# Keeping the exchange buffers of one more batch on chip in a fused Fourier-mixing and mixture-of-experts kernel

## The chip, the cores and the metric

The kernel runs on one core of a Trainium2 chip. The metric is the device time of one execution in microseconds (us); lower is better. The kernel before takes 1597.15 us, the median of three runs (1596.53 to 1599.73). Its trace comes from a further execution under the profiler, which took longer: 1614.27 us, of which 1612.5 us lie between the first and the last instruction. All times below that carry a position ("at 131.87") are positions in that trace.

## The reference

Two layers in a row, all in float32. The first multiplies each batch (2496 tokens of 256 numbers, 8 batches) by a filter in the frequency domain. The second sends each of the 19968 tokens to the one of 8 experts with the largest gate logit.

```python
# x: (8, 2496, 256), filt: (1249, 256), w_gate: (256, 8), w1: (8, 256, 1024), w2: (8, 1024, 256)
X = np.fft.rfft(x, axis=1)
y = np.fft.irfft(X * (filt_r + 1j * filt_i)[None], n=2496, axis=1)
t = y.reshape(19968, 256)
logits = t @ w_gate
e = argmax(logits, axis=1)                 # one expert for each token
gate = softmax(logits)[e]
out = gate * (relu(t @ w1[e]) @ w2[e])
```

## The kernel before

A batch's Fourier transform of length 2496 = 39 x 64 is done as four sets of small matrix products, which the kernel calls stages. Stage A transforms along 39 (tokens on the partitions), stage B along 64 and then multiplies by the filter, stage C transforms back along 64, stage D back along 39. Between A and B, and between C and D, the data change their layout. For batches 1 to 7 this is done by way of DRAM: the result of A is stored to `zd` and loaded again in another order, the result of C likewise through `ud`.

```python
def load_z(b, c):                          # DRAM -> SBUF, ahead of stage B
    f0, n = FH[c]
    zi = fin(("z", b, c))
    nc.sync.dma_start(out=zi[:HP, :n], in_=zd[b][:, f0:f0 + n, :])
    nc.sync.dma_start(out=zi[HP:, :n], in_=zd[b][:, NF + f0:NF + f0 + n, :])

def stage_a(b, c):                         # two groups of tokens per product
    ...
    for j in range(0, n, 2):
        p = bank()
        mm(p[:TK, :], lhsT=tas, rhs=xt[:TP, j:j + 2, :], start=True, stop=True)
        evac(zo[:, j:j + 2, :], ...)       # PSUM -> SBUF, on VectorE or ScalarE
    for r, m, v in columns(zd[b], i0, n):
        move(v, zo[:r, m])                 # SBUF -> DRAM

def stage_b(b, f):
    c, j = divmod(f, 4)
    if b == 0:
        zi, j = outs.pop(("zi", f)), 0
    else:
        zi = ins["z", b, c] if j == 0 else ins.pop(("z", b, c))
    p = bank()
    mm(p, lhsT=tbs, rhs=zi[:, j:j + 2, :], start=True, stop=True)
    ...
    nc.vector.tensor_mul(ys, z2, ht[:, f:f + 2, :])
    nc.vector.scalar_tensor_tensor(out=yw[:HP], in0=z2[HP:], scalar=-1.0, in1=fi, ...)
    nc.vector.tensor_mul(yw[HP:], z2[:HP], fi)
    (nc.gpsimd if b == 0 else nc.vector).tensor_tensor(ys, ys, yw, op=ALU.add)
```

Stage C is one product of 512 columns per step and ends in `move` to `ud`; stage D reads `ud` back through `load_u`.

Batch 0 is treated differently: its data stay in SBUF, in two buffers `zt` and `ut`, and the layout is changed by TensorE transposes against the identity.

```python
def first_a(c):                            # stage A of batch 0
    ...
    for j in range(0, n, 2):
        p = bank()[:, :4 * TK]
        for h in range(DH):
            for i in range(2):
                mm(p[...], lhsT=xt[:TP, j + i, h * P:(h + 1) * P], rhs=tas, start=True, stop=True)
        for h in range(DH):
            evac(zv[:, h], pv[:, h], 2 * TK)             # into zt

def turn_z(f):                             # between A and B of batch 0
    ...
    for i in range(2):
        for h in range(DH):
            nc.tensor.transpose(p[:, i, h, :], zu["z"][:, h, f + i]..., ident)
    evac(zi, p..., 2 * D)

def first_c(f):                            # stage C of batch 0: four products of 128 columns
    ...
    for h in range(DH):
        evac(zu["u"][:, h, :, :, f:f + 2], ..., D)       # into ut

def turn_u(c):                             # between C and D of batch 0: four transposes, one evac
    ...
```

After stage D of a batch, its logits are taken (`turn_y`, `logits`, `turn_logits`), its tokens are routed on VectorE (`route`) and scattered by GpSimd to a DRAM list sorted by expert (`rows`). The experts read 256 or 512 rows of that list at a time (`turn_x`, `hidden` or `hidden_by_quarters`, `result`), with the weights of that expert loaded for each such tile. For tiles of 512 rows GpSimd adds blocks of the rows (`sums`) and of the weights (`wsum`) first.

The program is built by a list of steps. Slot k holds stages B and C of batch k, stage A of batch k + 1 and stage D of batch k - 1. Steps of the experts are put between those of the slots by an estimate of time that the builder keeps. The order on each engine is then fixed. The experts' SBUF pool takes the place of batch 0's pool `pro`, so it opens when batch 0 has done with it, in slot 1:

```python
def experts_pool():
    first.close()
    pools["moe"] = ctx.enter_context(tc.tile_pool(name="moe", bufs=2, side="right", reuse_waits="tile"))

# in slot(k), for k > 0
    for c in range(nch + 3):
        at = 0.45 * c / (nch + 3) - 0.1 if k == 1 else 0.2 + 0.8 * c / (nch + 3)
        if c < nch and k == 1:
            steps.append((at - 0.05, lambda c=c: turn_u(c), None, 0.22 * CH[c][1]))
        ...
        if k == 1 and c == nch:
            steps.append((at, experts_pool, None, 0.0))
    steps.append((0.38 if k == 1 else 2.0, lambda: begin_route(k - 1), None, 0.0))
```

Lines of the kernel that the profile names: L413 `first_a`, L430 `turn_z`, L438 `first_c`, L453 `turn_u`, L337 `stage_a`, L351 the product of `stage_b` and L358 to L362 its filter, L372 `stage_c`, L391 and L395 `stage_d`, L466 `turn_y`, L480 `logits`, L491 `turn_logits`, L537 and L538 products of `route`, L596 the scatter to `rows`, L727 `turn_x`, L743 to L746 `wsum`, L765 `hidden_by_quarters`, L806 `hidden`, L821 `result`, L227 every `evac`.

Of the kernel before, what the change touches and what calls it, by code (L numbers as in the profile page):

```python
# [10 lines left out]
F32 = mybir.dt.float32  # L11
# [8 lines left out]
P = 128  # L20
S = 2496
D = 256
# [5 lines left out]
N2 = 64  # L28
# [90 lines left out]
def kernel(  # L119
# [174 lines left out]
    ins, outs, lgs, yts = {}, {}, {}, {}  # L294
    NIN, YB = 7, 6

    moves, stored = [[], []], set()

    def move(o, i):
# [43 lines left out]

    def stage_b(b, f):
        c, j = divmod(f, 4)
        if b == 0:
            zi, j = outs.pop(("zi", f)), 0
        else:
            zi = ins["z", b, c] if j == 0 else ins.pop(("z", b, c))
        p = bank()  # L350
        mm(p, lhsT=tbs, rhs=zi[:, j:j + 2, :], start=True, stop=True)  # L351

        z2 = p.rearrange("p (i d) -> p i d", i=2)
        ys = outs["y", b, f] = sb.tile([P, 2, D], F32, tag="ys", name="ys", bufs=3)
        yw = (pro if b == 0 else sb).tile([P, 2, D], F32, tag="yw", name="yw", bufs=2 if b == 0 else 1)
        half, f1 = divmod(f, NF // 2)
        fi = ht[half * HP:(half + 1) * HP, NF + f1:NF + f1 + 2, :]
        nc.vector.tensor_mul(ys, z2, ht[:, f:f + 2, :])  # L358
        nc.vector.scalar_tensor_tensor(out=yw[:HP], in0=z2[HP:], scalar=-1.0, in1=fi, op0=ALU.mult, op1=ALU.mult)
        nc.vector.tensor_mul(yw[HP:], z2[:HP], fi)  # L360

        (nc.gpsimd if b == 0 else nc.vector).tensor_tensor(ys, ys, yw, op=ALU.add)  # L362
        free["v"] = max(free["v"], now[0]) + (2.1 if b == 0 else 2.8)
# [17 lines left out]
    def stage_d(b, c):  # L381
        if c == 0:
            lgs[b] = sb.tile([TP, NG, E], F32, tag="lg", name="lg")
        i0, n = CH[c]
        held_y[0] += 1
        ui = outs.pop(("ui", c)) if b == 0 else ins.pop(("u", b, c))
        yo = outs["o", b, c] = sb.tile([P, 4, DR], F32, tag="y", name="yo", bufs=YB)[:TP]
        for j in range(0, n, 2):
            p = bank()
            if i0 + j + 2 < NG:  # L390
                mm(p[:TP, :], lhsT=tds, rhs=ui[:TK, j:j + 2, :], start=True, stop=True)  # L391
            else:

                for i, k in enumerate((TK, NS)):
                    mm(p[:TP, i * D:(i + 1) * D], lhsT=tds[:k, :], rhs=ui[:k, j + i, :], start=True, stop=True)  # L395
            evac(yo[:, j:j + 2, :D], p[:TP, :].rearrange("p (i d) -> p i d", i=2), 512)
# [2 lines left out]

    zu = {}  # L400

    def first_a(c):
        i0, n = CH[c]
        xt = ins.pop(("x", 0, c))
        if c == 0:

            zu["z"] = pro.tile([P, DH, NF, 2, N2], F32, name="zt", bufs=1)
            zu["u"] = pro.tile([P, DH, N2, 2, NF], F32, name="ut", bufs=1)
        for j in range(0, n, 2):
            p = bank()[:, :4 * TK]  # L410
            for h in range(DH):
                for i in range(2):
                    mm(p[:, (2 * h + i) * TK:(2 * h + i + 1) * TK], lhsT=xt[:TP, j + i, h * P:(h + 1) * P], rhs=tas,  # L413
                       start=True, stop=True)
            t0 = NB * (i0 + j)
            m = min(2 * NB, N2 - t0)
            pv = p.rearrange("p (h t c f) -> p h c f t", h=DH, c=2, f=NF)[:, :, :, :, :m]
            zv = zu["z"].rearrange("p h f c t -> p h c f t")[:, :, :, :, t0:t0 + m]
            for h in range(DH):
                evac(zv[:, h], pv[:, h], 2 * TK)  # L420

    def turn_z(f):
        if f % 4 == 0:
            nc.scalar.copy(out=ht[HP:, f:f + 4], in_=ht[:HP, f:f + 4])
            free["s"] = max(free["s"], now[0]) + 1.1
        zi = outs["zi", f] = pro.tile([P, 2, D], F32, tag="zi", name="zi")
        p = bank().rearrange("p (i h d) -> p i h d", i=2, h=DH)
        for i in range(2):
            for h in range(DH):
                nc.tensor.transpose(p[:, i, h, :], zu["z"][:, h, f + i].rearrange("p c t -> p (c t)"), ident)  # L430
        evac(zi, p.rearrange("p i h d -> p i (h d)"), 2 * D)

    def first_c(f):
        ys = outs.pop(("y", 0, f))
        p = bank().rearrange("p (h i c t) -> p h i c t", h=DH, c=2, i=2)
        for i in range(2):
            for h in range(DH):
                mm(p[:, h, i].rearrange("p c t -> p (c t)"), lhsT=ys[:, i, h * P:(h + 1) * P],  # L438
                   rhs=tcs, start=True, stop=True)
        for h in range(DH):  # L440
            evac(zu["u"][:, h, :, :, f:f + 2], p[:, h].rearrange("p i c t -> p t c i"), D)

    def turn_u(c):
        i0, n = CH[c]
        ui = outs["ui", c] = pro.tile([P, 4, D], F32, tag="ui", name="ui")
        for j in range(0, n, 2):
            p = bank().rearrange("p (i h d) -> p i h d", i=2, h=DH)
            whole = i0 + j + 2 < NG
            for i in range(2):
                t0 = NB * (i0 + j + i)  # L450
                m = min(NB, N2 - t0)
                for h in range(DH):
                    nc.tensor.transpose(  # L453
                        p[:m * NS, i, h, :], zu["u"][:, h, t0:t0 + m].rearrange("p t c f -> p (t c f)"), ident)
                if not whole:
                    evac(ui[:m * NS, j + i, :], p[:m * NS, i].rearrange("p h d -> p (h d)"), D)
            if whole:
                evac(ui[:TK, j:j + 2], p[:TK].rearrange("p i h d -> p i (h d)"), 2 * D)
# [380 lines left out]
    def slot(k):  # L839

        steps, nch = [], len(CH)
        if k == 0:
            steps.append((0.4, load_rest, None, 0.0))
            for f in range(-2, NF + 2, 2):
                at = (f + 2) / (NF + 4)
                if 0 <= f < NF:
                    steps.append((at, lambda f=f: stage_b(k, f), None, 0.85))
                if f + 2 < NF:
                    steps.append((at + 0.01, lambda f=f: turn_z(f + 2), None, 0.44))
                if f >= 2:  # L850
                    steps.append((at + 0.02, lambda f=f: first_c(f - 2), None, 0.85))
        elif k < B:
            for f in range(0, NF + 2, 2):
                at = f / (NF + 2)
                if f < NF:
                    steps.append((at, lambda f=f: stage_b(k, f), ("z", k, f // 4) if f % 4 == 0 else None, 0.85))
                if f >= 2:
                    steps.append((at + 0.01, lambda f=f: stage_c(k, f - 2), None, 0.85))
        if k + 1 < B:
            for c in range(nch):  # L860
                steps.append(((0.25 if k == 0 else 0.0) + 0.7 * c / nch, lambda c=c: stage_a(k + 1, c), ("x", k + 1, c), 0.43 * CH[c][1]))
        if k > 0:
            for c in range(nch + 3):
                at = 0.45 * c / (nch + 3) - 0.1 if k == 1 else 0.2 + 0.8 * c / (nch + 3)
                if c < nch and k == 1:
                    steps.append((at - 0.05, lambda c=c: turn_u(c), None, 0.22 * CH[c][1]))
                if c < nch:
                    steps.append((at, lambda c=c: stage_d(k - 1, c), ("u", k - 1, c) if k > 1 else "y", 0.43 * CH[c][1]))
                if c >= 3 and c % 2:
                    steps.append((at + 0.01, lambda c=c: logits(k - 1, (c - 3) // 2), None, 0.9))  # L870
                if 1 <= c <= nch:
                    steps.append((at + 0.03, lambda c=c: turn_y(k - 1, c - 1), None, 0.22 * CH[c - 1][1]))
                if c >= 3 and c % 2:
                    later = at + (0.07 if k == 1 else 0.11)
                    steps.append((later, lambda c=c: turn_logits(k - 1), None, 0.25))
                    steps.append((later + 0.001, lambda c=c: sides.append(route(k - 1, (c - 3) // 2)), None, 0.0))
                if k == 1 and c == nch:
                    steps.append((at, experts_pool, None, 0.0))
            steps.append((0.38 if k == 1 else 2.0, lambda: begin_route(k - 1), None, 0.0))
        return sorted(steps, key=lambda step: step[0])  # L880

    STEPS = [(0.0, lambda: load_filters(0), None, 0.0)]
    for c in range(len(CH)):
        STEPS.append((0.0, lambda c=c: first_a(c), ("x", 0, c), 0.43 * CH[c][1]))
        if c + 1 < len(FH):
            STEPS.append((0.0, lambda c=c: load_filters(c + 1), None, 0.0))
    SLOT = []
# [182 lines left out]
```

## Time and profile before

| what | value |
|---|---|
| time, median of 3 | 1597.15 us |
| span of the profiled execution | 1612.5 us |
| TensorE, matmul records | 1536.1 us, 95%, 7432 records |
| VectorE / ScalarE / GpSimd busy | 43% / 33% / 38% |
| moved by DMA | 287.50 MB, 178 GB/s over the span |
| `fin<-zd`, `zd<-zo`, `ud<-uo`, `fin<-ud` | loads and stores of the exchange, 7 batches |

A float32 product appears as two matmul records, a transpose as one. The records of one engine can overlap, since a product starts before the last one has drained; a record's duration is therefore longer than the time by which it moves the next one back. "Waited for" names what released an engine after it stood idle. PE is TensorE, PEld its weight loads, DVE VectorE, ACT ScalarE, POOL GpSimd, SP the queue from which the DMAs are issued.

### The profile page before, as it was taken

How to read it: one execution, taken by the hardware profiler on the slowest of the kernel's cores; microseconds unless marked ns; L12 is line 12 of the kernel's file. 1: busy time of each engine (PE TensorE's matmuls, PEld its weight loads, DVE VectorE, ACT ScalarE, POOL GpSimd, SP SyncE). 2: the span in 40 equal slices, each digit the busy share in tenths (PEclk: the TensorE clock that was granted, in tenths of full speed). 3: DMA queues.
4: the chain of work that ended last, by engine and by line, in shares of the span. 5: the costliest groups of instructions: out<-in, count | busy, mean ns of one | idle time of the engine just before them, and what ended most of it. 6: DMA issues, size and time to landing. Idle time of an engine off the chain costs nothing. (4 is left out here: it accounts for less than half of the span.)

```text
span 1612.5 us, 23212 instructions
## 1 busy us (share of the span) xinstructions
PE 1536.1 (95%) x7432; PEld 1211.1 (75%) x7432; DVE 694.7 (43%) x1797; ACT 533.5 (33%) x1106; POOL 608.5 (38%) x715
## 2 busy tenths in 40 slices
PE   7988898999999999999999899988999999999998
PEld 5533556667678767887688687877888888899997
DVE  4676562443756565357646354336343420000000
ACT  4434342343332333333333332222322223333433
POOL 4132324213634553455435555564444411111111
PEclk9999898999999999999999999999999999999999
DMA  8669695596784485446634633343344447665561
GB/s 245 166 193 300 217 328 164 180 314 217 206 264 142 153 270 156 121 139 163 195 116 141 165 127 115 116 160 102 99 165 139 164 144 249 194 230 179 171 190 34
DMA packets 119276, 287.50 MB, mean 178 GB/s; under 512 B 17587, under 2 KB 58812, under 8 KB 119157
## 3 DMA queue, kind: packets, MB, share of 16 engines
q1 hardware_dynamic: 99941, 242.69, 49.7%
q0 software_dynamic: 19216, 43.33, 7.9%
q8 instruction: 61, 1.00, 0.3%
q14 instruction: 58, 0.48, 0.1%
HBM read 205.95 MB, written 80.90 MB: 178 GB/s over the span
## 5 line engine op out<-in xcount | busy, mean ns | idle before, releaser
L821 PE MATMUL bank<-w2t,hT 128*128 128x256 f32 x2240 | 500.3, 380 | 0.2 <-ACT part L778 0.2
L821 PEld LDWEIGHTS bank<-w2t,hT 128*128 128x128 f32 x2240 | 424.8, 190 | 75.9 <-issue 17.2
L827 POOL DMA_INDIRECT out_dram<-ys,idt x163 | 160.8, 986 | 610.8 <-ACT ys L826 326.4
L596 POOL DMA_INDIRECT rows<-yo,row x176 | 175.0, 994 | 223.1 <-issue 54.5
L826 ACT ACTIVATE ys<-bank,gts 128x256 f32<-128x256 f32 x161 | 76.2, 474 | 425.9 <-PE bank L821 348.1
L773 ACT ACTIVATE hT<-hT 128x1024 f32<-128x1024 f32 x112 | 113.7, 1052 | 292.9 <-DVE hT L769 253.2
L806 PE MATMUL bank<-xT,w1t 128*128 128x128 f32 (+1 forms) x1184 | 191.9, 317 | 0.3 <-issue 0.3
L765 PE MATMUL bank<-sums,wsum 128*128 128x256 f32 x672 | 165.9, 393 | 19.4 <-POOL wsum L744 7.7
L806 PEld LDWEIGHTS bank<-xT,w1t 128*128 128x128 f32 x1184 | 169.3, 193 | 20.0 <-issue 9.3
L765 PEld LDWEIGHTS bank<-sums,wsum 128*128 128x128 f32 x672 | 129.7, 197 | 50.4 <-issue 10.5
L769 DVE TENSOR_TENSOR hT<-bank,part 128x512 f32<-128x512 f32 x168 | 115.6, 688 | 117.5 <-ACT part L778 63.0
L227 DVE COPY xT<-bank 128x128 f32<-128x128 f32 (+2 forms) x46 | 20.2, 439 | 286.1 <-PE bank L727 264.0
L812 ACT ACTIVATE hT<-bank 128x128 f32<-128x128 f32 (+1 forms) x295 | 93.4, 318 | 81.7 <-PE bank L806 68.2
L765 PE MATMUL bank<-xT,w1t 128*128 128x256 f32 x448 | 108.5, 386 | 0.4 <-ACT yo L227 0.4
L358 DVE TENSOR_TENSOR ys<-bank,ht 128x512 f32<-128x512 f32 x80 | 55.0, 688 | 100.4 <-PE bank L351 68.6
L765 PEld LDWEIGHTS bank<-xT,w1t 128*128 128x128 f32 x448 | 83.7, 193 | 15.3 <-issue 3.3
L372 PE MATMUL bank<-ys,tcs 128*128 128x512 f32 x140 | 75.3, 620 | 12.5 <-DVE ys L362 8.5
L769 DVE TENSOR_TENSOR part<-bank,part 128x512 f32<-128x512 f32 x112 | 76.7, 685 | 18.0 <-PE bank L765 14.5
L821 PE MATMUL bank<-w2s,hT 128*128 x368 | 83.2, 379 | 0.0
L743 POOL TENSOR_TENSOR wsum<-w1t 128x256 f32<-128x256 f32 x56 | 41.8, 747 | 106.4 <-PE bank L765 99.2
L769 DVE TENSOR_TENSOR hT<-bank,hT 128x512 f32<-128x512 f32 x112 | 76.8, 685 | 8.9 <-PE bank L765 4.2
L391 PE MATMUL bank<-fin,tds 120*117 120x512 f32 x140 | 69.6, 620 | 7.4 <-DMA fin<-ud 7.4
(152 smaller groups left out, 1813.2 us busy)
## 6 DMA issues: line engine op xcount, KB each, us to landing
w1t<-in_moe_w_dram SPq DMA_DIRECT2D x130, 512.0 KB
w2t<-in_moe_w_dram SPq DMA_DIRECT2D x84, 512.0 KB
fin<-in_x_dram SPq DMA_DIRECT2D x40, 512.0 KB
fin<-zd SPq DMA_DIRECT2D x70, 256.0 KB
ud<-uo SPq DMA_DIRECT2D x70, 256.0 KB
zd<-zo SPq DMA_DIRECT2D x35, 480.0 KB
fin<-ud SPq DMA_DIRECT2D x35, 480.0 KB
xg<-rows SPq DMA_DIRECT2D x28, 544.0 KB
```

The costliest lines, as they stand in the source:

```text
L358: nc.vector.tensor_mul(ys, z2, ht[:, f:f + 2, :])
L372: mm(p, lhsT=tcs, rhs=ys, start=True, stop=True)
L391: mm(p[:TP, :], lhsT=tds, rhs=ui[:TK, j:j + 2, :], start=True, stop=True)
L596: sc = nc.gpsimd.indirect_dma_start(out=rowsd, out_offset=bass.IndirectOffsetOnAxis(ap=at, axis=0), in_=what, in_offset=None,)
L765: mm(q[:, v], lhsT=left[:, v * P:(v + 1) * P], rhs=right, start=True, stop=True)
L769: nc.vector.tensor_tensor(o, q, a, op=ALU.add)
L773: nc.scalar.activation(o, q, AF.Relu)
L806: mm(p[:, :m], lhsT=w1t[2 * i + g][:, dh, fh, v * P:(v + 1) * P], rhs=xts[i][:, dh, :m], start=(dh == 0), stop=(dh == DH - 1))
L812: lambda: nc.scalar.activation(hT, p[:, :m], AF.Relu))
L821: mm(p[:, :D], lhsT=hs[i][k % 4 // 2][:, k // 4, k % 2, j // 2, j % 2 * P:(j % 2 + 1) * P], rhs=w2, start=(k == 0), stop=(k == FT - 1))
L826: lambda: nc.scalar.activation(ys, p[:, :D], AF.Copy, scale=gate))
L827: nc.gpsimd.indirect_dma_start(out=out, out_offset=bass.IndirectOffsetOnAxis(ap=idt[i].bitcast(U32)[:, j, :], axis=0), in_=ys, in_offset=None,
```

## The change

Batch 1 is treated as batch 0 was: its data stay in SBUF between the stages, and no longer pass through `zd` and `ud`. The two buffers `zt` and `ut` become three of the same size that are taken by turns: z of batch 0, u of batch 0, z of batch 1, and u of batch 1 in the place of z of batch 0. Since the pool `pro` is needed one batch longer, the experts' pool opens in slot 2 instead of slot 1, and the tile list of batch 0 is made then too. The purpose is to spare the early part of the kernel four passes of a batch through DRAM. The sum in the filter step stays on VectorE for batch 1.

```diff
+    CHIP = 2
 def stage_b(b, f):
-        if b == 0:
-            zi, j = outs.pop(("zi", f)), 0
+        if b < CHIP:
+            zi, j = outs.pop(("zi", b, f)), 0
...
-        yw = (pro if b == 0 else sb).tile([P, 2, D], F32, tag="yw", name="yw", bufs=2 if b == 0 else 1)
+        yw = (pro if b < CHIP else sb).tile([P, 2, D], F32, tag="yw", name="yw", bufs=2 if b < CHIP else 1)
...
+    def exchange(name, b):
+        zu[name, b] = pro.tile([P, DH * N2 * NS], F32, tag="zu", name=name, bufs=3)
...
-            zu["z"] = pro.tile([P, DH, NF, 2, N2], F32, name="zt", bufs=1)
-            zu["u"] = pro.tile([P, DH, N2, 2, NF], F32, name="ut", bufs=1)
+            exchange("z", b)
...
 (first_a, turn_z, first_c and turn_u take the batch as an argument; first_c opens u at f == 0)
...
 def slot(k):
         if k == 0:
             steps.append((0.4, load_rest, None, 0.0))
+        if k < CHIP:
             for f in range(-2, NF + 2, 2):
...
-                steps.append((..., lambda c=c: stage_a(k + 1, c), ("x", k + 1, c), 0.43 * CH[c][1]))
+                steps.append((..., lambda c=c: (first_a if k + 1 < CHIP else stage_a)(k + 1, c), ("x", k + 1, c), ...))
         if k > 0:
+            soon = k <= CHIP
             for c in range(nch + 3):
-                at = 0.45 * c / (nch + 3) - 0.1 if k == 1 else 0.2 + 0.8 * c / (nch + 3)
-                if c < nch and k == 1:
+                at = 0.45 * c / (nch + 3) - 0.1 if soon else 0.2 + 0.8 * c / (nch + 3)
+                if c < nch and soon:
...
-                if k == 1 and c == nch:
+                if k == CHIP and c == nch:
                     steps.append((at, experts_pool, None, 0.0))
+                    for b in range(CHIP - 1):
+                        steps.append((at + 0.001, lambda b=b: begin_route(b), None, 0.0))
-            steps.append((0.38 if k == 1 else 2.0, lambda: begin_route(k - 1), None, 0.0))
+            if k >= CHIP:
+                steps.append((0.45 if k == CHIP else 2.0, lambda: begin_route(k - 1), None, 0.0))
```

## The prediction

> **What bounds the kernel now.** I read the page first. Its first line says that TensorE is the engine that counts:
>
> ```profile
> PE 1536.1 (95%) x7432; PEld 1211.1 (75%) x7432; DVE 694.7 (43%) x1797; ACT 533.5 (33%) x1106; POOL 608.5 (38%) x715
> ```
>
> But 95% is a share of records that overlap. The timeline of TensorE gives what a step really takes from it: the distance from one start to the next where nothing waits.
>
> ```profile
> 33.48 1.02 PE L351 MATMUL bank<-zi,tbs 128*128 128x512 f32 x2
> 34.35 0.60 PE L430 MATMUL bank<-ident,zt 128*128 128x128 f32 x4
> 34.78 1.06 PE L438 MATMUL bank<-tcs,ys 128*128 128x128 f32 x8
> 35.67 1.88 PE L337 MATMUL bank<-fin,tas 117*120 117x512 f32 x4
> 37.39 1.02 PE L351 MATMUL bank<-zi,tbs 128*128 128x512 f32 x2
> ```
>
> A product of 512 columns (2 records) costs 34.35 - 33.48 = 0.87 us, four transposes 0.43, four products of 128 columns (8 records) 0.89, two products of stage A 1.72. Likewise the timeline gives 0.216 us for each record of 256 columns, 0.112 for one of 128 or 120, 0.100 for a transpose of 117 columns, 0.87 for the eight transposes of L453, and 0.059 for a record of L480. I multiply these by the instruction lists of the program, in their order, and cut at the last stage C product of each batch. All products together need 1486 us; the span is 1612.5. About 126 us are waits, a slow clock after them, and the two ends, and only those can be won. The view by windows, cut at the same places (columns: length, busy PE, PEld, DVE, ACT, POOL, granted clock, DMA share, GB/s), shows where they lie:
>
> ```profile
> 0.00:55.30 55.30, 45.24 (x249) 32.71 (x250) 30.32 (x56) 25.19 (x47) 23.96 (x32) 1.00 0.74 205
> 55.30:119.60 64.30, 54.93 (x234) 28.01 (x234) 44.27 (x104) 25.11 (x50) 13.03 (x13) 0.96 0.72 194
> 119.60:189.10 69.50, 59.46 (x216) 30.81 (x214) 39.53 (x121) 27.86 (x58) 17.00 (x18) 0.89 0.88 279
> 189.10:309.50 120.40, 108.78 (x453) 75.51 (x452) 58.51 (x199) 41.37 (x87) 41.20 (x45) 0.93 0.68 211
> 309.50:418.50 109.00, 105.03 (x465) 73.40 (x464) 54.62 (x161) 40.04 (x89) 37.70 (x41) 0.98 0.80 247
> 418.50:892.30 473.80, 467.61 (x2160) 359.57 (x2159) 271.75 (x637) 154.86 (x271) 224.28 (x268) 1.00 0.58 173
> 892.30:1105.00 212.70, 193.72 (x922) 160.44 (x921) 90.37 (x240) 58.35 (x100) 118.71 (x143) 0.96 0.42 131
> 1105.00:1612.50 507.50, 501.35 (x2744) 450.64 (x2742) 105.36 (x281) 160.72 (x409) 132.60 (x159) 1.00 0.50 162
> ```
>
> Window lengths less the work in them: slot 0 55.3 - 41.2 = 14.1 (5.3 of it before the first product), slot 1 64.3 - 49.3 = 15.0, slot 2 69.5 - 49.9 = 19.6, slot 3 120.4 - 99.0 = 21.4, slot 4 109.0 - 101.5 = 7.5. Slots 5 to 7 lose 13, the rest 36. The change can reach the first five: 78 us. What ends the waits there (waits of PE, first 400 us):
>
> ```profile
> PE bank L372 <- DVE ys L362: 7.8, 6, 2.7
> PE bank L765 <- POOL wsum L744: 7.7, 2, 4.7
> PE rk L537 <- DVE oe L526: 6.7, 2, 3.4
> PE bank L413 <- DMA fin<-in_x_dram: 5.3, 1, 5.3
> PE bank L727 <- DMA xg<-rows: 4.0, 1, 4.0
> PE bank L391 <- DMA fin<-ud: 2.2, 1, 2.2
> ```
>
> The reader is to see that DRAM exchange itself ends one wait of 2.2 us. More is lost to VectorE's filter and to the first expert tiles. Each wait is followed by slow products:
>
> ```profile
> 131.87 3.61 PE L391 MATMUL bank<-fin,tds 120*117 120x512 f32 x4 [2.20 <-DMA fin<-ud]
> 249.55 5.48 PE L765 MATMUL bank<-sums,wsum 128*128 128x256 f32 x12 [4.66 <-POOL wsum L744]
> ```
>
> Four records of 512 columns take 1.88 us elsewhere (L337 above), here 3.61.
>
> **What the Trainium skill says.** Perfetto Trace Analysis, section Identifying the Most-Contended Engine: busy time of matmuls is no measure of how near TensorE is to its limit, since pipelined instructions overlap. The trace agrees (1536 us busy, some 1486 of work), which is why I use start-to-start times. TensorE: Matmul & The Clock Gate, section What's actually happening: after an idle window of about 3.4 us the clock falls to half, and comes back after about as long of work. The trace agrees in kind (3.61 against 1.88 us above), though there the wait just before was only 2.20 us. The same page, section Part 4: PE-mode transpose: the result goes to PSUM and has to be copied out, and a transpose of 128x128 took about 275 ns; here the record of L430 lasts 274 ns, but the next one starts 109 ns later.
>
> **The change part by part.** *TensorE, added.* `turn_z`: 40 transposes at 0.109 = 4.4 us. `turn_u`: 44 at 0.109 = 4.8. `first_a`: 88 records at 0.112 = 9.9, in place of 22 at 0.429 = 9.4: +0.5. `first_c`: 80 at 0.112 = 9.0 in place of 20 at 0.429 = 8.6: +0.4. Stages B and D cost the same. Sum: 10.1 us and 210 more records. It is work on the engine that bounds.
>
> *DMA, removed.* z and u of one batch, 64 x 40 x 256 x 4 bytes each, stored and loaded: 4 x 2.62 = 10.5 MB. In the first 189 us the windows move 11.3 + 12.5 + 19.4 = 43 MB, so a quarter goes, and most of the direct wait of L391 (2.2 us plus 1.7 of slow clock).
>
> *ScalarE and VectorE.* 10 more evictions for `zi` at 0.587 us, 12 for `ui`, 20 of 256 elements at 0.425 instead of 10 of 0.585, 22 of 240 instead of 11 of 512. By the instruction lists VectorE gets 5 more and ScalarE 38 more: about 16 us on ScalarE, which is busy 25 of 64 us in slot 1. Beside other work.
>
> *What moves.* In the new order the first expert products come near the end of slot 2 (3.0 us of them before the last stage C of batch 2, against 5.6 before), after batch 1's scatter. The first tile of 512 rows comes with stages of batches 2 and 3 between its products, and on GpSimd its `sums` and `wsum` stand together, where before eight scatters of about 1.3 us each stood among them. The expert work by the end of slot 4 is the same in both, 115.8 us.
>
> *Slot by slot.* I take the length of a stretch from its like in the trace before. Slot 0: work 41.6, 55.5 us. Slot 1: work 54.0. Its second half is paced by VectorE: four filter operations of 0.69 to 0.72, 2.8 us per step, and the same number as before; the seven steps from 92.9 to 119.6 took 26.7 us with 18 of TensorE work in them, so the 3 us of new transposes there are free, and those in the first half are not: 66.5 us. Slot 2: work 52.7, like slot 1 before (49.3 in 64.3), with the 3 us of experts in VectorE's shadow: 64 us. It ends at 186 instead of 189.1. Slot 3: work 104.4. Of the loss of 21.4 I drop the two `wsum` waits in part (7.7 to 3), half of the slow clock after them (2 to 3), and the part due to late loads: 13 stays, 117.5 us. Slot 4: work 98.1 + 5 = 103. Sum: 406.5 against 418.5 with equal expert work done. That is 12 us; after it nothing differs by design. I take off 3 for ScalarE (second rival). 1597.15 - 9 = 1588.
>
> **Rivals.** *First, VectorE and routing keep the pace, and the added work is paid in full.* For it: `ys` L362 leads the waits, DMA ends only a small part of them, and the experts, which fill holes, come later. Then slots 1 and 2 last some 70 us each and 10 us are given away: 1603 to 1607. Against it: TensorE has 15 to 20 us of slack in each of the slots 1 to 3. *Second, ScalarE becomes the limit at the start of slot 2.* In the new order nearly all evictions of `ui`, `yo`, `yt` and `zo` there go to ScalarE, in pairs on one engine, some 25 us of them against 32 of TensorE work, in a chain of transposes, eviction, product, eviction. It would cost 3 to 8 us: 1591 to 1597. *Third, everything early is relieved.* DMA is busy 88% in slot 2 and clock is at 0.89; if the loss of slots 1 to 4 (63 us) fell to 25, the gain would be 38 - 10 = 28: 1569. Against it: the filter's waits and those of routing (`oe` L526, 6.7) stay by the lists. *Fourth, the last third shifts.* From 892 to 1105 waits cost some 25 us, two of 5.8 and 4.7 us before L765. The new order shifts them by a few us either way, with no rule that I can read.
>
> **Range and chances.** The first rival and the third are 1605 and 1569; the fourth adds 6 either way. 8 in 10: 1573 to 1603. Faster by over 2% needs less than 1565, past the third rival: 0.04. Slower by over 2% needs more than 1629, 24 us beyond the first: 0.01. Within 2%: 0.95.
>
> **What would show it.** Right: 277 MB moved and 7642 records; no `fin<-ud` wait at the first L391; last stage C of batch 2 near 186 and of batch 4 near 406; wait for `wsum` about 3 us; the stretch after the last stage C of batch 7, which was 720 us and gets 3.5 us more of expert work, within 8 us of 724. The step on slots 1 and 2 is wrong if these two together last over 138 us or under 125; that on slot 3 if its loss is still 20. The whole is wrong if the loss saved early comes back after slot 4, or if ScalarE ends more than 6 us of TensorE's waits in slot 2.

## The result and the profile after

The changed kernel takes 1623.29 us (median of 4; 1622.63 to 1624.43) where the kernel before takes 1597.16 us beside it: ratio 1.0161, 95% interval 1.0144 to 1.0179. It is 26 us slower; 1588 with a range of 1573 to 1603 had been predicted. The same program takes from 1597 to 1615 us from one chip and occasion to the next, so every ratio below is to the kernel before on the same chip in the same set of runs.

In the new kernel most lines stand 13 further down: L339 `stage_a`, L353 product of `stage_b`, L360 to L364 its filter, L374 `stage_c`, L393 `stage_d`, L424 `first_a`, L441 `turn_z`, L451 `first_c`, L466 `turn_u`, L527 to L551 `route`, L609 the scatter, L701 the load of `xg`, L740 `turn_x`, L746 to L749 `sums`, L756 to L759 `wsum`, L778 `hidden_by_quarters`, L834 `result`, L839 and L840 its eviction and the store of output rows.

The page of the changed kernel, totals and DMA:

```profile
PE 1541.9 (95%) x7642; PEld 1230.9 (76%) x7642; DVE 704.1 (43%) x1802; ACT 547.4 (34%) x1144; POOL 608.3 (37%) x715
DMA packets 112358, 277.03 MB, mean 171 GB/s; under 512 B 17067, under 2 KB 53172, under 8 KB 112237
```

Exactly 7642 records and 277 MB: what is added and removed was counted rightly. The view by windows, cut at the last stage C product of batches 0 to 4 and 7 (the sixth window is slots 5 to 7), with the columns of the prediction:

```profile
0.00:56.80 56.80, 46.85 (x316) 39.66 (x316) 31.08 (x60) 25.29 (x54) 23.93 (x32) 1.00 0.69 204
56.80:121.80 65.00, 58.77 (x333) 37.47 (x332) 46.21 (x112) 31.20 (x68) 16.73 (x16) 0.99 0.35 100
121.80:188.60 66.80, 59.45 (x254) 32.42 (x254) 41.11 (x132) 33.34 (x70) 16.85 (x17) 0.94 0.61 184
188.60:312.40 123.80, 111.36 (x475) 77.02 (x475) 55.55 (x168) 42.61 (x88) 33.48 (x39) 0.94 0.74 227
312.40:421.20 108.80, 101.84 (x449) 71.03 (x449) 59.19 (x172) 41.73 (x90) 45.03 (x49) 0.97 0.77 248
421.20:888.90 467.70, 462.80 (x2144) 356.95 (x2143) 271.08 (x638) 154.13 (x268) 222.32 (x266) 1.00 0.57 173
888.90:1110.00 221.10, 195.90 (x920) 162.71 (x919) 98.36 (x291) 56.23 (x96) 117.01 (x141) 0.94 0.42 130
1110.00:1622.70 512.70, 504.91 (x2758) 453.62 (x2758) 101.51 (x231) 162.88 (x411) 132.97 (x159) 1.00 0.49 160
```

DMA share in slots 1 and 2 falls from 0.72 and 0.88 to 0.35 and 0.61, and the clock there is better (0.99 and 0.94 against 0.96 and 0.89): the change does what it is for. But slots 3 and 4 are no shorter than they were, and what follows batch 7 takes 733.8 us instead of 720.2. Waits of PE in the first 430 us of the changed kernel (us in total, times, longest):

```profile
PE rk L550 <- DVE oe L539: 10.1, 2, 6.0
PE bank L740 <- DMA xg<-rows: 6.6, 1, 6.6
PE bank L424 <- DMA fin<-in_x_dram: 5.3, 1, 5.3
PE bank L353 <- DMA fin<-zd: 4.2, 1, 4.2
...
PE bank L393 <- DMA fin<-ud: 0.7, 1, 0.7
```

The filter `ys` and `wsum`, 7.8 and 7.7 us in the first 400 us before, have left the head of the list. In their place stand `oe` of routing (which expert each token has), `xg<-rows` (the rows of an expert tile), and a wait for `fin<-zd` at the first stage B of batch 3, at 193.68.

### The profile page after: what moved, and what is told of

It reads as the page before. It is cut to its first block, busy times and chain, and to the rows that moved or that the text cites. A ratio compares the mean times of both kernels' runs of the same rounds, so it can differ in the third digit from the quotient of the medians.

```text
span 1622.7 us, 23599 instructions
## 1 busy us (share of the span) xinstructions
PE 1541.9 (95%) x7642; PEld 1230.9 (76%) x7642; DVE 704.1 (43%) x1802; ACT 547.4 (34%) x1144; POOL 608.3 (37%) x715
## 3 DMA queue, kind: packets, MB, share of 16 engines
q1 hardware_dynamic: 93021, 232.20, 46.7%
## 5 line engine op out<-in xcount | busy, mean ns | idle before, releaser
L834 PE MATMUL bank<-w2t,hT 128*128 128x256 f32 x2240 | 499.4, 380 | 0.2 <-ACT part L791 0.2
L834 PEld LDWEIGHTS bank<-w2t,hT 128*128 128x128 f32 x2240 | 424.1, 190 | 73.6 <-issue 14.9
L840 POOL DMA_INDIRECT out_dram<-ys,idt x163 | 160.7, 986 | 630.5 <-ACT ys L839 336.9
L609 POOL DMA_INDIRECT rows<-yo,row x176 | 176.3, 1002 | 200.8 <-issue 44.1
L839 ACT ACTIVATE ys<-bank,gts 128x256 f32<-128x256 f32 x161 | 76.3, 474 | 439.1 <-PE bank L834 375.7
L786 ACT ACTIVATE hT<-hT 128x1024 f32<-128x1024 f32 x112 | 114.1, 1051 | 284.2 <-DVE hT L782 284.2
L778 PE MATMUL bank<-sums,wsum 128*128 128x256 f32 x672 | 165.4, 392 | 19.5 <-POOL sums L747 11.8
L778 PEld LDWEIGHTS bank<-sums,wsum 128*128 128x128 f32 x672 | 129.6, 196 | 49.8 <-POOL sums L747 13.8
L778 PE MATMUL bank<-xT,w1t 128*128 128x256 f32 x448 | 108.9, 387 | 0.0
L778 PEld LDWEIGHTS bank<-xT,w1t 128*128 128x128 f32 x448 | 85.0, 195 | 15.8 <-issue 3.4
L360 DVE TENSOR_TENSOR ys<-bank,ht 128x512 f32<-128x512 f32 x80 | 55.0, 687 | 95.6 <-PE bank L353 95.0
L756 POOL TENSOR_TENSOR wsum<-w1t 128x256 f32<-128x256 f32 x56 | 41.0, 732 | 120.3 <-PE bank L778 120.0
L834 PE MATMUL bank<-w2s,hT 128*128 x368 | 83.2, 379 | 0.0
L782 DVE TENSOR_TENSOR hT<-bank,hT 128x512 f32<-128x512 f32 x112 | 76.7, 685 | 12.3 <-PE bank L778 10.3
L834 PEld LDWEIGHTS bank<-w2s,hT 128*128 128x128 f32 x368 | 68.2, 190 | 8.3
L353 PE MATMUL bank<-fin,tbs 128*128 128x512 f32 x120 | 63.8, 614 | 4.2 <-DMA fin<-zd 4.2
```

Of the source, the lines that this page charges most:

```text
L609: sc = nc.gpsimd.indirect_dma_start(out=rowsd, out_offset=bass.IndirectOffsetOnAxis(ap=at, axis=0), in_=what, in_offset=None,)
L756: nc.gpsimd.tensor_tensor(t[:, 0], w[:, 0, 1], w[:, 1, 1], op=ALU.add)
L778: mm(q[:, v], lhsT=left[:, v * P:(v + 1) * P], rhs=right, start=True, stop=True)
L782: nc.vector.tensor_tensor(o, q, a, op=ALU.add)
L786: nc.scalar.activation(o, q, AF.Relu)
L834: mm(p[:, :D], lhsT=hs[i][k % 4 // 2][:, k // 4, k % 2, j // 2, j % 2 * P:(j % 2 + 1) * P], rhs=w2, start=(k == 0), stop=(k == FT - 1))
```

## The experiments

In what follows "loss" is what it was in the prediction: the length of a stretch, to the last stage C product of its batch, less the TensorE work of the program in it.

| kernel | ratio to before | 95% interval | loss, slots 0-2 | slots 3-4 | slots 5-7 | rest |
|---|---|---|---|---|---|---|
| e1, before, another chip | 0.9990 | 0.9976 to 1.0004 | 49.4 | 26.5 | 15.4 | 30.9 |
| e2, later pool alone | 1.0043 | 1.0026 to 1.0059 | 45.1 | 40.4 | 15.9 | 32.3 |
| e3, changed, `turn_z` twice | 1.0154 | 1.0137 to 1.0171 | 46.7 | 34.1 | 19.7 | 41.4 |
| e4, before | 1.0004 | 0.9992 to 1.0017 | 44.6 | 22.3 | 9.8 | 37.1 |
| e5, changed | 1.0135 | 1.0107 to 1.0164 | 41.5 | 28.5 | 14.8 | 44.4 |
| e6, changed, old late order | 1.0063 | 1.0049 to 1.0077 | 41.4 | 31.8 | 9.4 | 31.5 |
| e7, before, new late order | 1.0070 | 1.0041 to 1.0100 | 45.9 | 24.9 | 11.0 | 43.3 |
| e8, e6 with a later first tile | 0.9997 | 0.9983 to 1.0010 | 42.3 | 27.9 | 14.6 | 30.6 |
| e9, e6, `turn_z` twice | 1.0097 | 1.0070 to 1.0124 | 44.6 | 35.2 | 12.6 | 33.0 |
| e10, before, `sums` on VectorE | 0.9943 | 0.9924 to 0.9962 | 50.6 | 18.1 | 9.3 | 29.0 |
| e11, changed, `sums` on VectorE | 1.0076 | 1.0048 to 1.0104 | 43.3 | 22.7 | 22.0 | 30.9 |
| e12, e8, `sums` on VectorE | 0.9970 | 0.9950 to 0.9990 | 40.5 | 22.3 | 7.3 | 27.9 |
| e13, e6, one tile's `wsum` on VectorE | 1.0032 | 1.0020 to 1.0043 | 40.5 | 24.1 | 8.7 | 31.2 |
| e14, e6 again | 1.0080 | 1.0066 to 1.0094 | 40.6 | 30.1 | 8.6 | 35.3 |

e1 to e3 shared a chip, so did e4 to e7, e8 to e11, and e13 and e14; e12 ran later on the chip of e1 to e3.

**e1: the kernel before, traced again.** No edit.

> The kernel before, unchanged, to get a trace of an execution that takes what the timed ones take: the first trace of it is 1614 us long, the timed executions 1597. All theories expect 1597 +- 2. Theory A (the late stretch is what differs from execution to execution): the stretch after the last stage C of batch 7 takes about 704 us here instead of 720, and everything before it ends within 2 us of the first trace. Theory B (the early, DRAM-fed stretch differs): batch 4's last stage C comes some 15 us earlier than 418.

Measured: the traced execution spans 1608.5 us, and the kernel takes 1613.4 us beside 1614.7 of its like, where 1597 had been expected. The loss lies where the first trace had it, with 4 us less of it behind batch 7. So the length of the first trace, 17 us over the timed 1597, is not something peculiar to one execution: there are chips and occasions on which this program takes that long.

**e2: only the later opening of the experts' pool**, batch 1 through DRAM as before.

```diff
-    CHIP = 2
+    CHIP, OPEN = 1, 2
-                if k == CHIP and c == nch:
-                    steps.append((at, experts_pool, None, 0.0))
+                if k == OPEN and c == nch:
+                    steps.append((0.2, experts_pool, None, 0.0))
 (the lists of tiles likewise with OPEN)
```

> Only the later opening of the experts' pool: batch 1 goes through DRAM as before, the pool opens in slot 2 and batch 0's list is made there. No transposes are added. If the later start of the experts is what costs time, this takes 1607 to 1620. If the added TensorE work and the new order of slots 1 and 2 are what costs, it takes 1595 to 1602.

Measured: 1.0043, some 7 us, between the two ranges that had been named. The later pool costs by itself, and where it costs is slots 3 and 4: loss 40.4 against 26.5 in e1, while behind slot 4 it is nearly that of e1 (48.2 and 46.3). The timeline of TensorE shows one cause, which the changed kernel does not have (the bracket is the wait before, and what ended it):

```profile
260.06 4.36 PE L778 MATMUL bank<-sums,wsum 128*128 128x256 f32 x12 [12.10 <-POOL wsum L757]
```

**e3: the changed kernel with batch 1's 40 transposes of z made twice**, into the same place.

```diff
-        for i in range(2):
+        for i in [0, 1] * (1 + b):
```

> The changed kernel with batch 1's 40 transposes between stages A and B made twice (the same result, written twice). 4.4 us of TensorE work more. If added TensorE work is paid in full, 1623 + 4 = 1627 to 1628. If it falls into waits on VectorE in slots 1 and 2, under 1625.

Measured: 1.0154, not to be told from the changed kernel's 1.0161 and 1.0135 on other chips; slot 1 took 74.7 us instead of 65.0. By itself this left open whether added transposes are paid; e9 repeats it.

**e4 and e5: before and changed kernel traced on one chip.** No edit.

> The kernel before once more, for a trace on the same chip as the next three (another chip gave 1614 for it instead of 1597). All theories: within 0.3% of the kernel before.

> The changed kernel, unchanged, for a trace on the same chip. All theories: 1.016 of the kernel before, +26 us.

Measured: 1600.4 and 1624.1 us; spans 1599.8 and 1625.3. The 25.5 us between the spans: 10.0 are work; loss in slots 0 to 2 is 3.1 lower, in slots 3 and 4 6.2 higher, and after slot 4 it is 12.3 higher. Slot 3 loses the same in both (18.3 and 17.9 us); what rises is slot 4, from 3.9 to 10.6. Nearly half of the damage is in the part where the prediction had "nothing differs by design".

**e6 and e7: the order after slot 4 exchanged.** The builder decides between a step of the transform and one of the experts by a balance of time, `credit`. When the last step of slot 4 has been placed the balance is -3.12 in the kernel before and -2.53 in the changed one; the expert work done is the same. This 0.6 us in an estimate gives another order: the expert work placed in slots 5, 6 and 7 is 100.3, 129.6 and 105.4 us before and 111.5, 126.2 and 94.2 after. e6 sets the balance of the changed kernel to the old value there, and e7 that of the kernel before to the new one.

```diff
+        if k == 4:
+            MARK = len(STEPS)
 ...
                 f = next(fs, None)
+                gone[0] += 1
 ...
+            if gone[0] == MARK:
+                gone[0] += 1000
+                credit = -3.12        # e7, in the kernel before: -2.53
             flush()
```

> The changed kernel, with one number of the builder's state (the credit of the experts) set at the end of slot 4 to what it is there in the kernel before: the order of all TensorE instructions from slot 5 to the end is then that of the kernel before; slots 0 to 4 are those of the changed kernel. If the loss comes from the order of slots 5 and later, which the change shifts by accident, this takes 10 to 16 us less than the changed kernel, 1.006 to 1.010. If it comes from slots 0 to 4 and the added work, it stays at 1.014 to 1.018.

> The reverse: the kernel before up to the end of slot 4, then the changed kernel's order of experts and stages in slots 5 and later. If the accidental order costs, this takes 10 to 16 us more than the kernel before, 1.006 to 1.010. If the loss is early, it is within 0.2% of it.

Measured: 12 us less than e5 (1612.1), and 11 us more than e4 (1611.7). The shift of the later order alone costs 11 to 12 us, in either kernel. PE waits from 870 to 1130 us, e5:

```profile
PE bank L778 <- POOL sums L747: 10.2, 3, 5.9
PE bank L393 <- DMA fin<-ud: 7.6, 1, 7.6
PE bank L778 <- ACT ys L839: 4.7, 1, 4.7
PE bank L778 <- DVE part L782: 2.8, 1, 2.8
```

and e6:

```profile
PE bank L778 <- POOL sums L747: 8.5, 2, 4.8
PE bank L393 <- DMA fin<-ud: 4.0, 1, 4.0
PE bank L778 <- ACT ys L839: 3.9, 1, 3.9
```

e7 has the four waits of e5 to within 0.3 us (10.4, 7.3, 4.7, 2.8), and e4 has three, like e6 (9.2, 5.9, 4.2). These waits differ by 6 to 9 us between the two orders; the rest of the 11 to 12 us they do not show. Besides, GpSimd's queue in e5 shows how such a wait arises:

```profile
1078.14 0.98 POOL L840 DMA_INDIRECT out_dram<-ys,idt  x1 [4.63 <-DVE hT L782]
1079.12 0.76 POOL L746 TENSOR_TENSOR sums<-xT 128x256 f32<-128x256 f32 x1
1079.95 0.72 POOL L747 TENSOR_TENSOR sums<-xT,sums 128x256 f32<-128x256 f32 x1
...
1080.73 4.27 PE L778 MATMUL bank<-sums,wsum 128*128 128x256 f32 x12 [4.01 <-POOL sums L747]
```

The additions stand behind a store that was itself held up, and TensorE waits 4 us for them, at the end of a chain over three engines.

**e8: the first tiles asked for later**, on top of e6. The builder lets a tile be asked for 4 us of its estimate after the last scatter of its batch; here 20 us for the first two batches.

```diff
-            rows_at[b] = free["p"] + 4.0
+            rows_at[b] = free["p"] + (20.0 if b < 2 else 4.0)
```

> As the changed kernel with the old order after slot 4 (1.006), but the builder takes the rows of batches 0 and 1 to be ready 16 us later, so that the first tile of 512 rows comes 30 TensorE instructions later. The order after slot 4 is again that of the kernel before. If the loss in slots 3 and 4 is the price of asking for that tile before its rows are scattered, the wait of 6 us for its rows goes and the time is 1.000 to 1.003. If the late opening of the pool costs in itself, it only changes place: 1.005 to 1.008.

Measured: 0.9997, the time of the kernel before. What this tile waits for is seen in the changed kernel, where the load goes out when the last rows have been scattered and takes 10.2 us to land, with the DMA engines busy for nine tenths of that time or more:

```profile
218.05 0.90 POOL L609 DMA_INDIRECT rows<-yo,row  x1 [0.30 <-issue]
...
225.33 0.37 SPq L701 DMA_DIRECT2D xg<-rows  x1
...
235.63 1.94 PE L740 MATMUL bank<-ident,xg 128*128 128x128 f32 x8 [6.58 <-DMA xg<-rows]
```

In e8 the tile comes at 247 without a wait, and two waits for `wsum` return, of 2.97 and 1.86 us:

```profile
247.35 1.09 PE L740 MATMUL bank<-ident,xg 128*128 128x128 f32 x8
...
253.64 4.54 PE L778 MATMUL bank<-sums,wsum 128*128 128x256 f32 x12 [2.97 <-POOL wsum L757]
...
263.94 4.54 PE L778 MATMUL bank<-sums,wsum 128*128 128x256 f32 x12 [1.86 <-POOL wsum L757]
```

But e8 also lacks the wait of 6 us for `oe` near 406, so its time does not tell the two prices apart. Its trace says where the loss went: in slot 4, which loses 4.4 us where e6 and e9 with the early tile lose 11.5 and 15.7; slot 3 loses 23.5, not less than theirs (20.3 and 19.5). e13 separates the two.

**e9: e6 with `turn_z` of batch 1 made twice** (the edits of e6 and e3).

> The changed kernel with the old order after slot 4 and with batch 1's 40 transposes between A and B made twice: 4.4 us of TensorE work more than 1.006. If added TensorE work in slot 1 is paid in full, 1.009; if it falls into the waits for the filter, as the prediction had it for the half of them, 1.006 to 1.007.

Measured: 1.0097 against 1.0063 and 1.0080 for e6: 3 to 5 us for 4.4 us of transposes, near the 1.009 of full payment, and slot 1 takes 72.8 us instead of 65.2. The intervals touch, so the time alone doesn't settle it; but slot 1, which is 63.8 to 65.5 us in all other kernels, before and changed, was lengthened by more than the added work both times. The change's own 4.7 us of work in slot 1 lengthened it by 1.7 us (63.8 in e4, 65.5 in e5): they fell into waits. That with them the room there is used up is argued from this; the doubled transposes also stand one behind the other ahead of the same eviction, which may lengthen the slot by itself.

**e10 and e11: `sums` on VectorE** in the kernel before and in the changed one; order on TensorE unchanged.

```diff
-            nc.gpsimd.tensor_tensor(t[:, 0], b[:, 0, 1], b[:, 0, 0], op=ALU.subtract)
+            nc.vector.tensor_tensor(t[:, 0], b[:, 0, 1], b[:, 0, 0], op=ALU.subtract)
 (the other three lines likewise)
```

> The kernel before with the four sums of rows per 512-row tile on VectorE instead of GpSimd; the order on TensorE is the same. If GpSimd's queue, in which these sums stand behind scatters and stores, makes the waits of the late stretch, those 9 us and the slow clock after them go: 0.990 to 0.995. If the rows themselves or the weights come late, it is within 0.2% of the kernel before.

> The same edit in the changed kernel, whose waits of the late stretch are longer. If these waits are what the new order of slots 5 and later costs, it takes about 10 us (the added products) more than the kernel before with that edit: 0.996 to 1.003. If not, it stays at about 1.014.

Measured: the kernel before gains 0.6% (1599.8 us beside 1610.8), and this is the fastest version against its like. The changed one stays at 1.0076, where 0.996 to 1.003 was expected, so that guess was wrong: the late waits for `sums` do go (rest 30.9), but slots 5 to 7 lose 22. Of PE's waits in e11 from 421 to 1130 us these stand among the first four:

```profile
PE bank L374 <- DVE ys L364: 5.1, 3, 2.9
PE bank L778 <- ACT ys L839: 4.9, 1, 4.9
PE bank L778 <- DVE part L782: 3.8, 2, 2.9
```

The filter is back in the list, since VectorE has the additions as well. The new order keeps its price and pays it elsewhere; why in slot 6 above all (11.7 us) stays open.

**e12: the three repairs so far together**, e8 with `sums` on VectorE.

> The changed kernel with all three repairs: the order after slot 4 of the kernel before, the first tile of 512 rows asked for 16 us later by the builder's estimate, and the blocks of the rows added on VectorE. If the repairs add up, 0.9997 x 0.9943 = 0.994 of the kernel before, some 9 us less, and then the change itself is worth nothing once its order is mended, since the kernel before gains as much with the sums on VectorE alone. If keeping batch 1 on chip does pay when nothing stands in its way, under 0.991. If the sums on VectorE take from the changed kernel what they took when its late order was in force (the loss in slots 5 to 7 rose to 22 us there), 0.998 or more.

Measured: 0.9970; the profiled execution spans 1593.9 us. It beats both kernels, but gains less than the 0.994 that the repairs would add up to, and no more than e10, the kernel before with one of these repairs (0.9943). Set beside e10 and e8, keeping batch 1 on chip brings nothing that could be measured even in good order. Whether a later first tile would help the kernel before as well was not tried.

**e13 and e14: `wsum` of one tile on VectorE, and e6 again as its measure.**

```diff
+        add = nc.vector if [h // 2] == [i for i, a in enumerate(work) if a[0] == 4][1:2] else nc.gpsimd
-        nc.gpsimd.tensor_tensor(t[:, 0], w[:, 0, 1], w[:, 1, 1], op=ALU.add)
+        add.tensor_tensor(t[:, 0], w[:, 0, 1], w[:, 1, 1], op=ALU.add)
 (the other three lines likewise)
```

> The changed kernel with the old order after slot 4, and of the second tile of 512 rows alone the eight additions of wsum on VectorE instead of GpSimd; order on TensorE and on every queue otherwise as in that kernel. Theory 'lock': at 398 to 408 one VectorE operation of routing (two operands in SBUF) lasted 6.87 us instead of 0.22, as long as twelve additions of GpSimd stood without a gap, and TensorE waited 6.1 to 6.8 us for oe behind it. With only four additions left on GpSimd there the operation lasts at most 3 us, the wait for oe near 406 falls to under 4 us, and the time falls by 3 to 6 us: 1.0025 to 1.0045 of the kernel before, where the kernel with the old order has 1.0063. Rival 'rows': the whole price in slots 3 and 4 is the early load of the first tile (wait of 5.7 to 6.7 us at 235), which this leaves as it is: the time stays within 2 us of the kernel with the old order, 1.005 to 1.0075.

> The changed kernel with the old order after slot 4 again, on the chip of the run beside it, as its measure: 1.0063 of the kernel before under every theory (1.0049 to 1.0077 the first time), and the operation of 6.87 us at about 400 again.

Measured: 1.0032 against 1.0080; eight additions put on another engine bring 8 us, where 3 to 6 had been expected (5 beside the 1.0063 of e6). The timeline of e14, VectorE, GpSimd and TensorE:

```profile
396.97 0.77 POOL L746 TENSOR_TENSOR sums<-xT 128x256 f32<-128x256 f32 x1
397.20 0.63 DVE L527 TENSOR_TENSOR oh<-lg,mx 117x64 f32<-117x64 f32 x1
397.65 0.76 POOL L756 TENSOR_TENSOR wsum<-w1t 128x256 f32<-128x256 f32 x1
397.75 6.87 DVE L529 TENSOR_TENSOR ex<-lg,mx 117x64 f32<-117x64 f32 x1
...
403.82 0.71 POOL L757 TENSOR_TENSOR wsum<-wsum,w1t 128x256 f32<-128x256 f32 x1
404.55 0.21 DVE L531 TENSOR_TENSOR oh<-oh,em 117x64 f32<-117x64 f32 x1
404.62 0.73 POOL L759 TENSOR_TENSOR wsum<-w1t,wsum 128x256 f32<-128x256 f32 x1
...
405.68 0.65 PE L550 MATMUL rk<-oe,tri 117*117 117x64 f32 x2 [6.07 <-DVE oe L539]
...
406.56 3.73 PE L778 MATMUL bank<-xT,w1t 128*128 128x256 f32 x8
```

A subtraction of 0.22 us (the median of its 24 executions) begins while an addition of GpSimd runs, and ends when GpSimd's chain has its first gap, 404.53 to 404.62. The ten additions between 397.65 and 404.53 follow each other every 0.68 to 0.73 us, those of `sums` and of `wsum` mixed. TensorE waits 6.07 us and then works slowly (3.73 us for what takes 1.95 in e13). In e13:

```profile
398.51 0.21 DVE L529 TENSOR_TENSOR ex<-lg,mx 117x64 f32<-117x64 f32 x1
...
400.82 0.42 PE L550 MATMUL rk<-oe,tri 117*117 117x64 f32 x2 [0.55 <-DVE oe L539]
```

Here `sums` stands alone on GpSimd, L747 needs the result of L746 and begins 0.08 us after its end, and the subtraction comes in between. Loss of slot 4: 11.4 us in e14, 4.5 in e13, while the wait for `xg<-rows` stays (7.1 and 6.9). One operation of 6.87 us is there in the trace of the changed kernel, in e3, e5, e6, e9 and e14, all of them with the early first tile and with `sums` and `wsum` on GpSimd; it is not there in e1, e2, e4, e7, e8, e10 to e13, nor in the first trace. Shorter ones of the kind are in most of these too, and come through in a gap likewise; in e11, on 35 elements, after 2.75 us instead of 0.18:

```profile
613.50 2.75 DVE L653 TENSOR_TENSOR past<-tau,end 1x35 f32<-1x35 f32 x1
615.47 0.72 POOL L757 TENSOR_TENSOR wsum<-wsum,w1t 128x256 f32<-128x256 f32 x1
616.28 0.72 POOL L759 TENSOR_TENSOR wsum<-w1t,wsum 128x256 f32<-128x256 f32 x1
```

## Why the prediction was wrong

What the slots became, beside the forecast (us):

| slot | forecast | changed kernel | e13 |
|---|---|---|---|
| 0 | 55.5 | 56.8 | 57.0 |
| 1 | 66.5 | 65.0 | 65.0 |
| 2 | 64 | 66.8 | 66.8 |
| 3 | 117.5 | 123.8 | 124.0 |
| 4 | 103 | 108.8 | 102.6 |

**The added work, 10.1 us: right, and paid in full in the order that the change gave.** With some 2 us of expert work moved out of slot 2, work in slots 0 to 2 grows by 7.9 us, and the same slots are 4.8 us longer in e5 than in e4 (189.8 and 185.0 us), so 3.1 fell into waits. That "the 3 us of new transposes there are free" held for slot 1. But over the whole kernel nothing is left of this: e6 has as much loss as e4 (114.1 and 113.8 us in all) and is longer by just the work. That is the first rival's price, 1603 to 1607, and not its path: it had slots 1 and 2 at some 70 us each, and they last 65.0 and 66.8. And it is not a rule: e8 does the same 10 us more work and takes as long as the kernel before.

**The DMA, and slots 0 to 2: right in kind, too hopeful in size.** They were to end at 186 instead of 189.1, and end at 188.6. No wait for `fin<-ud` at the first stage D of batch 1; slots 1 and 2 together 131.8 us, inside the 125 to 138 that was set. ScalarE's `ui` and `u` end about 3 us of TensorE's waits there, under the 6 that would have spoken for the second rival.

**What could be won: too large.** "The change can reach the first five: 78 us" came from a trace that was 17 us longer than the timed runs, and the gain was then taken off the timed 1597. In e4, at 1600, the same slots lose 67 and slot 4 ends at 407.7, so that the forecast of 406.5 was to win 1 us there and not 12. The saving in slots 0 to 2 is 3 us there (44.6 to 41.5). It is larger where the kernel before loses more: 9 between the first trace and that of the changed kernel (49.7 to 40.3), 7 to 8 on the chip of e8 to e11 (50.6 in e10, 43.3 in e11, 42.3 in e8). The first trace being long is also why the two first traces differ by 10 us and the times by 26.

**Slot 3, "13 stays": failed, 19.4 stayed.** The `wsum` waits went, all of them where 3 us had been left, but TensorE now comes to the first tile of 512 rows while its load is under way (out at 225.33, landed 10.2 us later), and this wait took their place (6.6 us). In e4 and e5 the slot loses 18.3 and 17.9: one wait for another, and nothing won. The note under what would show it, that the step is wrong "if its loss is still 20", as good as came true.

**Slot 4, 103 with 5 us of loss: failed by 5.8 (10.7 us of loss), and for a reason that stood in the prediction as a benefit.** It says that on GpSimd "`sums` and `wsum` stand together, where before eight scatters of about 1.3 us each stood among them". It was said of the first tile of 512 rows; at the second, beside routing, the chain without gaps is what stopped VectorE for 6.87 us. Break it, and slot 4 is 102.6 us (e13). The Trainium skill (SBUF — State Buffer, section SBUF: two separate sides) states that VectorE and GpSimd share one pair of ports as an exclusive lock, which an operation of VectorE with two operands in SBUF needs too beside one of GpSimd that reads SBUF, and that the one that comes second blocks until the first is done. The traces agree that it is held up, and go further: here it stayed blocked through ten additions in a row, not one. The prediction asked how long each operation lasts, not which one it would stand beside.

**"After it nothing differs by design": failed, 12 us.** The design is the same; the order is not, because a balance of the builder differs by 0.6 us. The sign set for it, 724 us within 8 after batch 7, was missed with 733.8. The fourth rival had such a shift at 6 us either way, and it cost 11 to 12 (e6, e7). The waits at its end are shown; why this order is the worse one is argued only (stores before additions in GpSimd's queue), and e11 shows that moving those additions doesn't mend it.

From 9 us won by forecast to 25.5 lost between e4 and e5 it is 34.5 us: 10.8 because slots 0 to 4 were measured on a long trace, 14.3 because they ended at 420.8 instead of 406.5, 12.4 behind them, less the 3 that had been set aside for ScalarE. So the fourth rival came at twice its size, the first one's price came in another way than it had said, and the lock stood in none of them. That the early saving is given back was named as what would make the whole wrong.

## What to carry to other kernels

Against work added to an engine that is busy 95% of the span, set only waits that a trace of ordinary length shows. When a builder orders steps by an estimate, compare the order of the whole program, also behind the change, and undo the shift by itself before the change is judged. Look at which operations a new order puts side by side on VectorE and GpSimd: a chain without gaps on one can shut the other out, as here for 6.87 us. Two chains of dependent additions that leave gaps alone can leave none when they are mixed.

## What was not expected of the hardware

- An operation of VectorE on 117x64 elements with two operands in SBUF lasted 6.87 us instead of 0.22 beside ten additions of GpSimd that followed each other with no gap. A gap of 0.1 us, where one addition needed the result of the one before, was enough to let it through.
- The same kernel without change took 1597, 1600, 1611 and 1615 us in different sets of runs. The work is the same in all; the loss is 113.8 us at a span of 1599.8, 122.2 at 1608.5, 126.4 at 1612.5. It is not the chip alone: on the one of e1 to e3 it took 1614.7, and 1600.2 beside e12.
- The same four additions of 128x256 on VectorE instead of GpSimd made the kernel before 0.6% faster, though VectorE's filter is among the first of TensorE's waits.
